# Order of the first loads, clears and copies in a chunked attention and top-1 MoE kernel

## The chip, the cores and the metric

One core of a Trainium2 chip runs the whole program. The metric is the device time of one execution in microseconds (us), smaller is better; the number quoted for the kernel before is the median of three runs. The engines of the core are TensorE (PE in the profile, with PEld for its weight loads), VectorE (DVE), ScalarE (ACT), GpSimd (POOL) and SyncE (SP, which here only issues DMAs).

## What is computed

Attention in chunks of 32 queries, each over 8 memory keys and a window of the sequence, and then a mixture of experts in which each token goes to one of eight:

```python
for c in range(S // 32):                      # B 4, H 8, S 768, D 64
    l, r = max(0, 32*c - 16), min(S, 32*c + 32 + 8)
    k_full = concat(mem_k, k[:, :, l:r]); v_full = concat(mem_v, v[:, :, l:r])
    a = softmax(q[:, :, 32*c:32*c+32] @ k_full.T / sqrt(D))
    out[:, :, 32*c:32*c+32] = a @ v_full
x = out.transpose(0, 2, 1, 3).reshape(3072, 512)
e = argmax(x @ w_gate + modality_bias[modality_id])   # softmax gives the gate
y = gate * (relu(x @ w1[e]) @ w2[e])
```

## The kernel before

**Tiling.** The 32 pairs of batch and head are taken two at a time: 16 units of two heads, here called pairs 0 to 15 (`u` in the code). Each pair is done in two halves of twelve chunks (`hf`). For each pair there are a key tile `kbd` (two of them in turn: `kbds`), in which both heads' transposed keys stand as blocks with zeros beside them, and a value tile `vw` (three in turn: `vws`), 128 partitions with rows 0 to 63 for head 0 and rows 64 to 127 for head 1. In `vw` 56 rows of a head hold the window of a chunk and 8 rows the memory values; the blocks in which the one head's rows meet the other head's columns stay zero. They are cleared once for each of the three tiles, `vws[0]` and `vws[1]` half by VectorE (L136) and half by GpSimd (L154, L845), `vws[2]` wholly by GpSimd (L866). `edge_v` (L274) writes the column of ones that gives the softmax's sum, with the first and the last chunk apart.

**Loads.** `load_qk(u)` (L97) issues the keys' and the queries' load of a pair, 384 KB each. `load_v(u)` (L283) issues four loads for each head: the main one (L290, 184 KB, elements of 256 bytes), two small ones for the ends (L291, L292) and the memory values (L294 or L297). For pair 0 the memory values come from DRAM, spread over the chunks by the load itself; from pair 1 on they come from `spread_v`, two tiles in SBUF that VectorE fills with `spread_mem` (L193): `spread_mem(0)` in the prologue at L197, `spread_mem(1)` within `more_constants`. `mkp`, `mvr` and other small inputs go through ScalarE's queue.

**A pair's steps.** `trans_k` and `store_k` transpose the keys into `kbd` (PE, then two copies of 64 partitions for each head on ScalarE and VectorE); `mem_keys` (L327) puts the memory keys in, two copies on GpSimd, from `memT`, which VectorE copies from a transpose of `mk` at L851. `regroup_q`, `trans_q` and `store_q` do the same for queries. `scores`, `less_max` (maximum and subtraction on VectorE), `exps_t` (transposes, then the exponential on ScalarE) and `attend` follow for each half, then `normalize` on VectorE and `trans_x`. Before `attend`, `share_v` (L299) copies 24 rows of each window to the next chunk's place: eight copies of six chunks on GpSimd, head 0's four first, then head 1's four. The first half of a pair attends over chunks 0 to 11.

**Order.** On PE, SP and GpSimd instructions run in the order in which the program writes them; during the attention stage so do those of ScalarE and VectorE. The prologue stands at L843 to L868, the loop over the 32 halves at L872 to L956. In the loop the half `i` computes its scores while the half `i - 1` attends; `load_qk(u + 3)` and `load_v(u + 2)` stand at the end of a pair's first half. `pump` puts single steps of routing and of the constants between VectorE's other instructions. After the attention comes the mixture of experts, matmul after matmul on PE to the end.

Of the kernel before, what the change touches and what calls it, by code (L numbers as in the profile page):

```python
# [9 lines left out]
F32 = mybir.dt.float32  # L10
# [10 lines left out]
P = 128  # L21
B, H, S, D = 4, 8, 768, 64
NMEM = 8
NCH = S // 32
# [28 lines left out]
def tile_chunk_attention_top1_moe(  # L53
# [14 lines left out]
    nc = tc.nc  # L68
# [14 lines left out]
    ld = c_ld.enter_context(tc.tile_pool(name="ld", bufs=3))  # L83
# [3 lines left out]
    qf = q.rearrange("b h s d -> (b h s) d")  # L87
    kf = k.rearrange("b h s d -> (b h s) d")
# [3 lines left out]
    def bank():  # L92
        return ps.tile([P, 512], F32, name="tr", tag="tr", bufs=4)

    q2s, k2s = {}, {}

    def load_qk(u):  # L97
        r0 = u * 2 * S
        q2s[u] = ld.tile([P, 2, 6 * D], F32, name="q2")
        k2s[u] = ld.tile([P, 2, 6 * D], F32, name="k2")  # L100
        for t, f in ((k2s[u], kf), (q2s[u], qf)):
            nc.sync.dma_start(t, f[r0:r0 + 2 * S].rearrange("(h p j) d -> p h (j d)", p=P, j=6))

    man = ExitStack()
    man.enter_context(tc.manual_schedule(engines={mybir.EngineType.Activation, mybir.EngineType.DVE}))
# [20 lines left out]
    vws = [pers.tile([P, 2, NCH, D + 1], F32, name=f"vw{i}") for i in range(NVW)]  # L126
# [3 lines left out]
    zero = const.tile([P, 1], F32, name="zero")  # L130
# [62 lines left out]
    def spread_mem(i):  # L193
        nc.vector.memset(spread_v[i][:, :, D:D + 1], 1.0)
        nc.vector.tensor_copy(spread_v[i][:, :, 0:D], mvr[:, i:i + 1].to_broadcast([P, NCH, D]))

    spread_mem(0)  # L197

    def more_constants():
        nc.vector.tensor_copy(iota, iota_i)  # L200
# [73 lines left out]
    def edge_v(i):  # L274
        t = vws[i]
        for h in range(2):
            r = slice(64 * h, 64 * h + 64)
            nc.gpsimd.memset(t[r, h, 1:NCH - 1, D:D + 1], 1.0)
            nc.gpsimd.tensor_copy(t[r, h, 0:NCH:NCH - 1], vedge[r])
# [3 lines left out]
    def load_v(u):  # L283
        vw = vws[u % NVW]
        for h in range(2):
            hh = 2 * u + h
            r0 = 64 * h

            src = bass.AP(tensor=vf.tensor, offset=(hh * S + 8) * D, ap=[[D, 32], [32 * D, NCH - 1], [1, D]])
            nc.sync.dma_start(vw[r0 + 24:r0 + 56, h, 0:NCH - 1, 0:D], src)  # L290
            nc.sync.dma_start(vw[r0 + 24:r0 + 48, h, NCH - 1, 0:D], vf[hh * S + S - 24:hh * S + S])  # L291
            nc.sync.dma_start(vw[r0 + 16:r0 + 24, h, 0, 0:D], vf[hh * S:hh * S + 8])  # L292
            if u == 0:
                nc.sync.dma_start(vw[r0 + 56:r0 + 64, h, :, 0:D], mvf[hh].unsqueeze(1).to_broadcast([NMEM, NCH, D]))  # L294
            else:
                m0 = NMEM * (hh % 16)
                nc.sync.dma_start(vw[r0 + 56:r0 + 64, h], spread_v[hh // 16][m0:m0 + NMEM])  # L297

    def share_v(u):  # L299

        vw = vws[u % NVW]
        for h in range(2):
            r0 = 64 * h
            for c in range(0, NCH - 1, 6):
                w = min(6, NCH - 1 - c)
                nc.gpsimd.tensor_copy(vw[r0:r0 + 24, h, c + 1:c + 1 + w, 0:D], vw[r0 + 32:r0 + 56, h, c:c + w, 0:D])  # L306

    def regroup_q(u):
# [13 lines left out]
    def store_q(u, j):  # L322
        if j == 0:
            qTs[u] = wk.tile([P, S], F32, name="qT")
        nc.scalar.copy(qTs[u].rearrange("p (s j) -> p s j", j=2)[:, :, j], qts.pop((u, j))[:, 0:384])

    def mem_keys(u, eng):  # L327
        for h in range(2):
            r = slice(64 * h, 64 * h + 64)
            eng.tensor_copy(kbds[u % 2][r, :, h, 56:64], memT[r, u:u + 1, :].to_broadcast([64, NCH, NMEM]))  # L330
# [13 lines left out]
    def store_k(u, h, j, copy):  # L344
        tt = kts[u, h][64 * j:64 * j + 64]
        win = bass.AP(tensor=tt.tensor, offset=tt.offset, ap=[list(tt.ap[0]), [16, NCH], [1, 28]])
        dst = kbds[u % 2][64 * h:64 * h + 64, :, h, 0:56]
        copy(dst.rearrange("p c (i j) -> p c i j", j=2)[:, :, :, j], win)  # L348
# [69 lines left out]
    def pump(k, pe=False):  # L418
        k *= KB if routing and routing[0][2] == B - 2 else 1
        while k > 0 and routing:  # L420
            g, wait, b, since = routing[0]
            if wait:
                if not pe or now[0] < since + (wait == "late" or b < B - 2) + (wait == "late" and b < B - 2):
                    return
                pe = False
            r = next(g, None)
            if r is None:
                routing.pop(0)
                return
            routing[0] = (g, r if r != "v" else "", b, now[0])  # L430
            k -= r == "v"
# [409 lines left out]


    edge_v(0)  # L843
    load_v(0)
    nc.gpsimd.memset(vws[1][64:P, 0], 0.0)  # L845
    edge_v(1)
    trans_k(0)
    t = bank()
    nc.tensor.transpose(t[:, 0:P], mk, ident)
    regroup_q(0)  # L850
    nc.vector.tensor_copy(memT.rearrange("p u m -> p (u m)"), t[:, 0:P])  # L851
    mem_keys(0, nc.gpsimd)
    for h in (1, 0):
        for j in range(2):
            store_k(0, h, j, nc.vector.tensor_copy if j else nc.scalar.copy)
    trans_q(0)
    for j in range(2):
        store_q(0, j)
    nc.vector.memset(kbds[1][0:64, :, 1], 0.0)
    load_qk(2)  # L860
    load_v(1)
    mem_keys(1, nc.gpsimd)
    share_v(0)
    nc.gpsimd.iota(iota_i, [[1, 192]], base=0, channel_multiplier=0)
    for h in range(2):
        nc.gpsimd.memset(vws[2][64 * h:64 * h + 64, 1 - h], 0.0)  # L866
    edge_v(2)
    load_v(2)  # L868

    units = [(u, hf) for u in range(NU) for hf in range(2)]  # L870
    n = len(units)
    for i in range(n + 2):  # L872
        live = i < n
        u, hf = units[i] if live else (NU, i % 2)
        now[0] = i
        if i == MAN:
            man.close()
        if live and i < n - 1:
            scores(u, hf)
        if 1 <= i <= n:  # L880
            exps_t(*units[i - 1])
        if live:
            less_max(u, hf)
            pump(1)
        if u + 1 < NU and hf == 0:
            trans_k(u + 1)
            regroup_q(u + 1)
            pump(3)
            store_k(u + 1, 1, 0, nc.scalar.copy)
            store_k(u + 1, 0, 0, nc.scalar.copy)  # L890
            store_k(u + 1, 0, 1, nc.scalar.copy)
            store_k(u + 1, 1, 1, nc.vector.tensor_copy)
            pump(3)
        elif u + 1 < NU:
            share_v(u + 1)
            if u + 2 < NU:
                mem_keys(u + 2, nc.gpsimd)
            trans_q(u + 1)
            store_q(u + 1, 0)
            store_q(u + 1, 1)  # L900
            pump(5)
        elif live:
            pump(5)
        first = i in (n - 3, n - 2)
        if first:
            trans_x(*units[i - 2])
        if i == n - 2:
            scores(*units[i + 1])
        if 1 <= i <= n:
            attend(*units[i - 1])  # L910
        if i == n:
            trans_x(*units[i - 2])
            trans(0)
            trans(1)
            conv(4)
            conv(5, nc.gpsimd)
            normalize(*units[i - 1])
            mm1(0)
        if i > n:
            mm1(1)  # L920
        if i >= 2 and not first and i != n:
            trans_x(*units[i - 2])
        if 1 <= i < n:
            normalize(*units[i - 1])
            pump(1)
        if i >= 2:
            u2, hf2 = units[i - 2]
            if hf2 == 1 and u2 % 4 == 3:
                routing.append((route(u2 // 4), True, u2 // 4, 0))
        if i == 1:  # L930
            routing.append((more_constants(), False, -1, 0))
        if i == 6:
            assert not routing
            bias_rows()
        if i < n:
            pump(1, True)
        if live and hf == 0:
            if u + 3 < NU:
                load_qk(u + 3)
            if u >= 1 and u - 1 + NVW < NU:  # L940
                load_v(u - 1 + NVW)
        if (u, hf) == (NU - 2, 1):
            while routing:
                pump(99, True)
            c_ld.close()
            xp = ctx.enter_context(tc.tile_pool(name="xp", bufs=1, side="right"))
            ix = xp.tile([P, 2], I32, name="ix")
            gx = xp.tile([P, 2], I32, name="gx")
            xg = [xp.tile([P, XW], F32, name=f"xg{t}") for t in range(2)]
            xth, xtl = [xp.tile([P, 4, 256 + NR], F32R, name=f"xt{i}") for i in range(2)]  # L950
            hh, hl = [xp.tile([P, 8, 256], F32R, name=f"h{i}") for i in range(2)]
            load_w(0, 0)
            gather(0)
        elif u == NU - 1:
            conv(2 * hf)
            conv(2 * hf + 1, nc.gpsimd)  # L956
# [165 lines left out]
```

## Time and profile before

| | us |
|---|---|
| median of three runs | 453.18 |
| lowest and highest run | 451.9, 453.71 |
| the profiled execution | 453.23 |
| its span, first to last instruction | 451.4 |
| PE busy | 422.2 |
| DVE busy | 312.6 |
| ACT busy | 260.4 |
| POOL busy | 199.3 |

The profile is one execution. Its span is 1.8 us shorter than that execution's time. "Busy" sums the time of an engine's instructions; an engine that is busy need not be the one that sets the end. In the time lines times are counted from the start of the span, and the bracket at a line's end is the idle time of that engine just before it and what ended it. The granted clock of TensorE is given as a share of its full 2.4 GHz; its lower level, 1.2 GHz, is 0.5.

### The profile page before, as it was taken

To read this page: it belongs to the slowest core of one execution; us is meant where nothing else is said; L and a number is where in the kernel's file an instruction comes from. 1 tells how busy PE (TensorE), PEld (TensorE's weight loads), DVE (VectorE), ACT (ScalarE), POOL (GpSimd) and SP (SyncE) were. 2 spreads that over 40 slices of the span, in tenths; PEclk is the share of its full clock that TensorE was granted. 3 is DMA by queue.
4 is the path that set the end of the run, shared out by engine and by line. 5 is a ranking of instruction groups with operands and counts; after the bars stand their busy time and mean duration, and the time that the engine had idled before them with its cause. 6 is when DMAs were issued, how large, how long until landed. Compare 5 with 4: busy or idle time off the path is not lost. (4 is left out here: it accounts for less than half of the span.)

```text
span 451.4 us, 11915 instructions
## 1 busy us (share of the span) xinstructions
PE 422.2 (94%) x4109; PEld 362.7 (80%) x4109; DVE 312.6 (69%) x756; ACT 260.4 (58%) x522; POOL 199.3 (44%) x376
## 2 busy tenths in 40 slices
PE   5979998998977898999999999999999999999993
PEld 2858786786756687989798998989898989898982
DVE  8699799799897699848456455857566675848430
ACT  5566776775646663747366455656565655657521
POOL 8977779789777833214042231313040404040201
PEclk9799999999999999999999999999999999999998
DMA  7798999999877502277187834202662201120101
GB/s 198 142 231 201 227 235 210 225 229 197 188 196 187 183 2 81 61 219 235 36 242 228 237 95 166 70 1 95 187 212 69 91 5 58 40 73 23 48 0 47
DMA packets 69570, 61.74 MB, mean 137 GB/s; under 512 B 30603, under 2 KB 59491, under 8 KB 69492
## 3 DMA queue, kind: packets, MB, share of 16 engines
q1 hardware_dynamic: 62480, 41.52, 37.8%
q0 software_dynamic: 5888, 19.11, 13.9%
q8 instruction: 36, 0.59, 0.6%
q14 instruction: 42, 0.34, 0.2%
q10 hardware_dynamic: 1124, 0.18, 0.2%
HBM read 76.02 MB, written 12.76 MB: 197 GB/s over the span
## 5 line engine op out<-in xcount | busy, mean ns | idle before, releaser
L778 PEld LDWEIGHTS tr<-xt,w 128*128 128x128 f32 x1152 | 141.0, 188 | 4.9 <-issue 2.7
L778 PE MATMUL tr<-xt,w 128*128 128x256 f32 (+1 forms) x1152 | 143.0, 284 | 1.9 <-PEq L1083 0.8
L788 PE MATMUL av<-wh,h 128*128 128x512 f32 x384 | 127.8, 399 | 0.0
L813 POOL DMA_INDIRECT out_dram<-o,ix_now x24 | 24.2, 1008 | 163.9 <-ACT o L809 161.9
L782 DVE SCALAR_TENSOR_TENSOR h<-tr,h 128x256 fp32r<-128x256 f32 x96 | 40.6, 423 | 71.6 <-ACT h L779 52.7
L788 PEld LDWEIGHTS av<-wh,h 128*128 128x128 f32 x384 | 72.3, 188 | 15.5 <-issue 0.4
L788 PE MATMUL av<-wl,h 128*128 128x512 f32 x192 | 75.6, 394 | 0.0
L306 POOL COPY vw<-vw 24x384 f32<-24x384 f32 (+1 forms) x128 | 61.0, 514 | 18.1 <-DMA vw<-in_v_dram 16.7
L725 DVE TENSOR_TENSOR wl<-raw,wh 128x512 fp32r<-128x512 f32 x91 | 63.0, 692 | 8.2 <-ACT wh L723 0.9
L779 ACT ACTIVATE h<-tr 128x256 fp32r<-128x256 f32 x96 | 36.8, 384 | 51.7 <-PE tr L778 30.5
L725 DVE TENSOR_TENSOR w<-raw,w 128x512 fp32r<-128x512 f32 x93 | 60.4, 695 | 5.0 <-ACT w L723 2.5
L723 ACT CAST wh<-raw 128x512 fp32r<-128x512 f32 x96 | 58.9, 615 | 2.0 <-DMA raw<-in_moe_w_dram 2.0
L723 ACT CAST w<-raw 128x512 fp32r<-128x512 f32 x96 | 53.6, 622 | 0.0
L809 ACT ACTIVATE o<-av,gate_now 128x512 f32<-128x512 f32 x24 | 16.2, 689 | 46.6 <-PE av L788 37.2
L788 PEld LDWEIGHTS av<-wl,h 128*128 128x128 f32 x192 | 36.2, 189 | 6.5
L348 ACT COPY kbd<-tr 64x672 f32<-64x672 f32 x47 | 36.6, 779 | 6.8 <-PE tr L342 5.8
L356 PE MATMUL sc<-kbd,qT 128*32 128x128 f32 x768 | 29.5, 290 | 2.9 <-POOL kbd L330 2.9
L740 POOL DMA_INDIRECT xg<-xd,gx x24 | 26.8, 1116 | 10.6 <-POOL gx L738 6.9
L376 ACT ACTIVATE PT<-tr 128x384 f32<-128x384 f32 x32 | 15.7, 492 | 25.8 <-PE tr L374 25.3
L386 PE MATMUL av<-vw,PT 128*32 128x130 f32 x768 | 28.3, 279 | 1.9 <-ACT PT L376 1.9
L761 ACT CAST xt<-tr 128x512 fp32r<-128x512 f32 x24 | 13.9, 587 | 24.3 <-PE tr L759 13.9
L356 PEld LDWEIGHTS sc<-kbd,qT 128*32 128x32 f32 x768 | 20.5, 115 | 8.4 <-issue 4.1
(245 smaller groups left out, 531.1 us busy)
## 6 DMA issues: line engine op xcount, KB each, us to landing
raw<-in_moe_w_dram SPq DMA_DIRECT2D x192, 256.0 KB
k<-in_k_dram SPq DMA_DIRECT2D x16, 384.0 KB
q<-in_q_dram SPq DMA_DIRECT2D x16, 384.0 KB
xd<-xb POOLq DMA_DIRECT2D x16, 384.0 KB, 5.6
vw<-in_v_dram SPq DMA_DIRECT2D x32, 184.0 KB
vw<-spread_v SPq DMA_DIRECT2D x30, 48.8 KB
vw<-in_v_dram SPq DMA_DIRECT2D x32, 6.0 KB
vw<-in_v_dram SPq DMA_DIRECT2D x32, 2.0 KB
```

Of the source, the lines that this page charges most:

```text
L306: nc.gpsimd.tensor_copy(vw[r0:r0 + 24, h, c + 1:c + 1 + w, 0:D], vw[r0 + 32:r0 + 56, h, c:c + w, 0:D])
L348: copy(dst.rearrange("p c (i j) -> p c i j", j=2)[:, :, :, j], win)
L356: nc.tensor.matmul(sc[32 * j:32 * j + 32, t * P:(t + 1) * P], qT[:, 32 * c:32 * c + 32], kbd[:, c].rearrange("p h m -> p (h m)"), start=Tr ...
L386: nc.tensor.matmul(avb[32 * j:32 * j + 32, t * W:(t + 1) * W], PT[:, t * P + 32 * j:t * P + 32 * j + 32], vw[:, :, c], start=True, stop=True,)
L723: nc.scalar.copy(wh[i], raw[i])
L725: (eng or nc.vector).tensor_sub(wl[i][:, s], raw[i][:, s], wh[i][:, s].bitcast(F32))
L740: nc.gpsimd.indirect_dma_start(out=xg[t], out_offset=None, in_=xd[0:rows], in_offset=bass.IndirectOffsetOnAxis(ap=gx[:, t:t + 1], axis=0))
L778: nc.tensor.matmul(pw, wt[f][:, c * P:(c + 1) * P], x[:, c, 0:w], start=(n == 0), stop=(n == 11))
L779: nc.scalar.activation(hh[:, f], ph, AF.Relu)
L782: nc.vector.scalar_tensor_tensor(hl[:, f], ph, 0.0, hh[:, f].bitcast(F32), op0=ALU.max, op1=ALU.subtract)
L788: nc.tensor.matmul(pos[t], x, w[8 + f], start=(f == 0 and n == 0), stop=(f == 7 and n == 2))
L813: nc.gpsimd.indirect_dma_start(out=out, out_offset=bass.IndirectOffsetOnAxis(ap=ix_now[:, t:t + 1], axis=0), in_=outs[t], in_offset=None, ...
```

## The change

In the prologue the order of the instructions changes:

- The keys of pair 2 are loaded ahead of the values of pair 0, its queries right behind these (both came together after the query copies of pair 0).
- On GpSimd `mem_keys(0)` comes ahead of the clearing of `vws[1]` and of `edge_v(1)`; `load_v(1)` follows `edge_v(1)`.
- The clearing of `vws[2]` is split: ScalarE clears rows 0 to 63 of head 1's columns by copying zeros, GpSimd the other half.
- `spread_mem(0)` leaves the prologue; it runs on VectorE in the loop's first pass, behind the key copies of pair 1, and `load_v(2)` is issued right behind it. Pair 1's memory values are therefore loaded from DRAM as pair 0's are.
- `share_v` alternates between the heads for each six chunks, in all pairs.

```diff
-    def load_qk(u):
+    def load_qk(u, parts=(0, 1)):
         r0 = u * 2 * S
-        q2s[u] = ld.tile([P, 2, 6 * D], F32, name="q2")
-        k2s[u] = ld.tile([P, 2, 6 * D], F32, name="k2")
-        for t, f in ((k2s[u], kf), (q2s[u], qf)):
-            nc.sync.dma_start(t, f[r0:r0 + 2 * S].rearrange("(h p j) d -> p h (j d)", p=P, j=6))
+        for i in parts:
+            tiles, f, name = ((k2s, kf, "k2"), (q2s, qf, "q2"))[i]
+            tiles[u] = ld.tile([P, 2, 6 * D], F32, name=name)
+            nc.sync.dma_start(tiles[u], f[r0:r0 + 2 * S].rearrange("(h p j) d -> p h (j d)", p=P, j=6))
...
-    spread_mem(0)
-
...
-            if u == 0:
+            if u < 2:
                 nc.sync.dma_start(vw[r0 + 56:r0 + 64, h, :, 0:D], mvf[hh].unsqueeze(1).to_broadcast([NMEM, NCH, D]))
...
-        for h in range(2):
-            r0 = 64 * h
-            for c in range(0, NCH - 1, 6):
-                w = min(6, NCH - 1 - c)
+        for c in range(0, NCH - 1, 6):
+            w = min(6, NCH - 1 - c)
+            for h in range(2):
+                r0 = 64 * h
                 nc.gpsimd.tensor_copy(vw[r0:r0 + 24, h, c + 1:c + 1 + w, 0:D], vw[r0 + 32:r0 + 56, h, c:c + w, 0:D])
...
     edge_v(0)
+    load_qk(2, (0,))
     load_v(0)
-    nc.gpsimd.memset(vws[1][64:P, 0], 0.0)
-    edge_v(1)
+    load_qk(2, (1,))
     trans_k(0)
...
     mem_keys(0, nc.gpsimd)
+    nc.gpsimd.memset(vws[1][64:P, 0], 0.0)
+    edge_v(1)
+    load_v(1)
     for h in (1, 0):
...
         store_q(0, j)
+    nc.scalar.copy(vws[2][0:64, 1], zero[0:64].unsqueeze(2).to_broadcast([64, NCH, D + 1]))
     nc.vector.memset(kbds[1][0:64, :, 1], 0.0)
-    load_qk(2)
-    load_v(1)
     mem_keys(1, nc.gpsimd)
     share_v(0)
     nc.gpsimd.iota(iota_i, [[1, 192]], base=0, channel_multiplier=0)
-    for h in range(2):
-        nc.gpsimd.memset(vws[2][64 * h:64 * h + 64, 1 - h], 0.0)
+    nc.gpsimd.memset(vws[2][64:P, 0], 0.0)
     edge_v(2)
-    load_v(2)
...
             store_k(u + 1, 1, 1, nc.vector.tensor_copy)
+            if u == 0:
+                spread_mem(0)
+                load_v(2)
             pump(3)
```

## Rows read from the trace of the kernel before

**Rows 1.** The page: PE's busy time, and its granted clock in 40 slices.
```profile
PE 422.2 (94%) x4109; PEld 362.7 (80%) x4109; DVE 312.6 (69%) x756; ACT 260.4 (58%) x522; POOL 199.3 (44%) x376
...
PEclk9799999999999999999999999999999999999998
```
**Rows 2.** Windows: stretch, busy time of each engine, PE's granted clock, DMA share, GB/s.
```profile
10.00:11.00 1.00, 0.00 (x0) 0.00 (x0) 1.00 (x1) 0.00 (x0) 0.81 (x4) 0.96 0.87 159
...
17.00:18.00 1.00, 1.00 (x7) 0.94 (x5) 0.56 (x1) 0.64 (x2) 0.96 (x2) 0.62 1.02 94
...
20.00:30.00 10.00, 8.60 (x156) 6.91 (x158) 9.66 (x39) 6.52 (x12) 9.55 (x21) 1.00 0.73 206
...
26.00:28.00 2.00, 1.42 (x28) 1.06 (x29) 1.96 (x9) 0.48 (x1) 1.88 (x6) 1.00 1.04 358
...
40.00:50.00 10.00, 10.00 (x176) 7.66 (x176) 8.46 (x23) 7.22 (x14) 5.86 (x12) 1.00 0.91 207
```
**Rows 3.** Time line of PE: start, duration, instruction, times; idle before it.
```profile
7.63 0.85 PE L320 MATMUL tr<-ident,qr 128*128 128x128 f32 x6 [1.01 <-DVE qr L311]
11.36 1.51 PE L356 MATMUL sc<-kbd,qT 128*32 128x128 f32 x24 [2.88 <-POOL kbd L330]
...
18.10 0.87 PE L386 MATMUL av<-vw,PT 128*32 128x130 f32 x24
...
24.33 0.87 PE L386 MATMUL av<-vw,PT 128*32 128x130 f32 x24
26.58 0.55 PE L408 MATMUL tr<-ident,xb 128*128 128x128 f32 x3 [1.38 <-DVE xb L401]
...
72.85 0.52 PE L408 MATMUL tr<-ident,xb 128*128 128x128 f32 x3 [1.64 <-DVE xb L401]
```
**Rows 4.** Time line of POOL, from the first edges to the second `share_v`.
```profile
7.87 0.29 POOL L279 COPY vw<-vedge 64x130 f32<-64x130 f32 x1
8.10 1.40 POOL L845 MEMSET vw<- 64x1560 f32 x1
...
10.57 1.54 POOL L330 COPY kbd<-memT 64x192 f32<-64x192 f32 x4
12.17 4.06 POOL L306 COPY vw<-vw 24x384 f32<-24x384 f32 x8
...
16.54 2.82 POOL L866 MEMSET vw<- 64x1560 f32 x2
...
20.45 4.83 POOL L306 COPY vw<-vw 24x384 f32<-24x384 f32 x8
```
**Rows 5.** Time line of DVE, the prologue, the third maximum and pair 5's queries.
```profile
6.03 0.92 DVE L195 COPY spread_v<-mvr 128x1536 f32<-128x1536 f32 x1
...
6.87 0.61 DVE L311 COPY qr<-q 128x768 f32<-128x768 f32 x1
...
7.71 1.75 DVE L348 COPY kbd<-tr 64x672 f32<-64x672 f32 x2
...
20.33 0.54 DVE L364 TENSOR_REDUCE mx<-sc 128x6 f32<-128x384 f32 x1
...
44.44 0.55 DVE L311 COPY qr<-q 128x768 f32<-128x768 f32 x1
```
**Rows 6.** Time line of ACT: the clearing of both key tiles, the first query copies.
```profile
2.54 2.84 ACT L134 COPY kbd<-zero 64x1536 f32<-64x1536 f32 x2
...
8.18 0.89 ACT L325 COPY qT<-tr 128x384 f32<-128x384 f32 x2 [0.59 <-PE tr L320]
```
**Rows 7.** Time line of SP, three of its DMA issues.
```profile
7.66 0.34 SPq L290 DMA_DIRECT2D vw<-in_v_dram  x1
...
13.36 0.28 SPq L292 DMA_DIRECT2D vw<-in_v_dram  x1
...
41.64 0.64 SPq L297 DMA_DIRECT2D vw<-spread_v  x1
```
**Rows 8.** Waits of SP from 4 to 27 us: in total, times, longest.
```profile
SPq L292 <- DMA vw<-in_v_dram: 0.5, 1, 0.5
```

## Prediction

> **What bounds the kernel now.** I read the page first: TensorE (PE) is busy 94% of the span and its clock falls below full only in the second of 40 slices, in the twelfth and in the last [rows 1]. The change touches only the first two of the sixteen head pairs, so the question is what sets the pace there, and whether time won there reaches the end. The view by windows answers the first half of it: the granted clock leaves 2.4 GHz within the 11th us (mean 0.96, so after about 0.92 of it) and comes back within the 18th (mean 0.62, so after 0.76 of it): some 6.8 us at 1.2 GHz, from 10.9 to 17.8 [rows 2]. VectorE (DVE) is busy 9.66 of the 10 us from 20 to 30; from 40 to 50 PE is busy all the time [rows 2].
>
> The time line of each engine then gives the chain. PE ends the first query transposes at 8.5, stands for 2.88 us until GpSimd (Pool) has put the memory keys into the first key tile, starts the first scores at 11.36, and gets to the first attend at 18.10 [rows 3]. Pool is late because `mem_keys(0)`, the first half of the four copies that start at 10.57, stands behind the clearing of `vws[1]` (1.40) and its edges, though what it needs, `memT`, is there by 7.71, where DVE's next instruction begins [rows 4, 5]. From 20.33 on DVE has hardly a pause, and PE waits for it at 26.58 [rows 2, 3, 5]. So: Pool's order until 11.4, PE at half clock until 18, DVE until about 40, PE after that. Whatever reaches DVE's row at 20.33 early reaches the end, unless a load is late.
>
> **The change part by part.**
>
> *The spread copy leaves DVE's front.* 0.92 us at 6.03 go [rows 5]. The regrouping of queries (0.61), `memT` (0.27, between the two rows shown) and two key copies (1.75) follow one behind the other, so the last copy ends at 9.46 - 0.76 = 8.7. ScalarE's two query copies (0.89, at 8.18 after 0.59 of idle) can start when ScalarE comes free at 7.6 and end by 8.6 [rows 6].
>
> *Memory keys first on Pool.* `edge_v(0)` ends at 8.16; `mem_keys(0)` is half of 1.54, 0.77 [rows 4]. It ends at 8.9, and the first scores start at 8.95 instead of 11.36: 2.4 us earlier. PE's pause of 2.88 shrinks to about 1.3. A pause of 1.38 (26.58) and one of 1.64 (72.85) left the clock at full [rows 1, 3], so I take it that it stays up. If it falls all the same, PE needs the 6.74 us that it needed before (11.36 to 18.10), and attends at 15.7.
>
> *Values and their copies.* What is swapped on Pool is a swap, so `share_v(0)` still starts near 12.17 [rows 4]. Its order changes: the second copy is now head 1's. In SP's time line the third value load of pair 1 stands still 0.5 us until 13.36, and what ends that is a value load [rows 7, 8]; I read it as head 1's main load of pair 0, the eighth issue before it. So Pool waits after one copy until 13.4. The third keys' load goes ahead of it: 384 KB that the DMA engines take over in a gap, since the values' issue at 7.66 waits for Pool's edges in any case, just as now [rows 4, 7]. I take 0.1 us for it; the bounds are 0 and the 1.1 us that these 384 KB need at the 358 GB/s of 26 to 28 us [rows 2]. One copy is 4.06 / 8 = 0.51. The first attend takes chunks 0 to 11, which are whole after four copies in the new order (six in the old): 13.5 + 3 x 0.51 = 15.0, at worst 16.1, against 18.10 now. With the half-clock case this is a gain of 2.0 to 3.1.
>
> *The spread copy in its new place* (0.92, on DVE, behind the last key copy of pair 1, about 12.8 to 13.7). Behind it on DVE stand the second maximum and subtraction, which PE wants after the first attend, so the Pool wait until 15.0 hides it; without that cover it costs 0.92. What the row of `share_v(1)` shows: eight copies took 4.83 instead of 4.06 where the other spread copy ran on DVE [rows 4], 0.77 more. The Trainium skill (SBUF — State Buffer, "Who interferes with whom") says of this that a DVE copy which uses both ports locks GpSimd out for the whole instruction, and speaks against the new place, beside the copies on which the attend now waits; the trace agrees with its 0.77. By the row the attend comes at up to 15.8, with a free Pool at 15.0; the copy lies mostly in Pool's wait for the load, so I take 0 and keep 0.77 as the bound.
>
> *DVE's chain.* The maximum at 20.33 starts 2.23 us after the first attend [rows 3, 5], which would make it 17.2. But between them stands the copy of `iota`, whose Pool half comes behind `share_v(0)`: 13.5 + 7 x 0.51 = 17.1, plus 0.2 between the rows at 12.17 and 16.54 for that instruction itself. With 0.4 for DVE's copies the maximum starts at 17.7: 2.6 us earlier. With the clock down it is 15.7 + 2.23 = 17.9, 2.4.
>
> *Pool later.* Half of the 2.82 us of clearing at 16.54 goes to ScalarE [rows 4]. Its cost there is half of 2.84, 1.42, behind the query copies (8.6 to 10.0) [rows 6]; next on ScalarE is the first key copy of pair 1, behind the first scores and the transposes after them, 8.95 plus half of 1.51 (half, at the full clock) and about as much again, 10.5: hidden, 0; uncovered, up to 1.4. Pool starts `share_v(1)` at 17.3 + 1.41 + 1.1 (edges: 20.45 less 19.36) = 19.8 instead of 20.45; four of eight copies (2.4) give 22.2 for the attend now at 24.33, half a microsecond after 24.33 - 2.6. PE's pause of 1.38 behind that attend covers it [rows 3].
>
> *Loads.* The pair-1 mem rows come from DRAM instead of the spread tile, 48 KB twice: between 0 and 0.4 us of DMA time, hidden before 19.8. The third values need Pool's clearing, which ends at 18.7 instead of 19.36 [rows 4], and the spread tile, ready at 13.7; the key loads behind them in SP's order move with them. From there on the DMA engines are full (share 1.04 from 26 us) [rows 2], so the stream of loads moves up by 0.7 us only while the engines move up by 2.6. The tightest load that I find is the query tile of pair 5: SP's wait for a query load ends at 41.64, DVE regroups at 44.44 [rows 5, 7]; 2.8 us of room, of which 1.9 is used. So the stream doesn't bind, but a gain over 3.5 would be cut there.
>
> **Sum.** 2.6 us, kept to the end: 453.23 of the profiled execution (span 451.4) - 2.6 = 450.6. The median of the runs is 453.18, so nothing has to be added.
>
> **The rivals.**
>
> *1. The clock falls in the new pauses and PE becomes the bound; slower.* From 11.36 to 18.10 PE did 6.74 us at half clock, so 3.4 at full; between 8.95 and the attend at 15.0 there are 6.05, so 2.7 us of pauses, and 3.8 if the third keys take their whole 1.1 us out of the values' time (attend at 16.1). After a pause of 2.88 the clock fell, after one of 1.64 it didn't, so it decides between these two [rows 3]. Another 6.8 us at 1.2 GHz then do 3.4 us less of PE's work: with the attend at 16.1 that is 3.4 - 2.0 = 1.4 us slower, 454.6, if nothing covers it. Against it: DVE is the bound from 20 on [rows 2], and covers most of it. What the rows show of the clock is that it fell after a pause and rose after steady work; the Trainium skill (TensorE: Matmul & The Clock Gate, "What's actually happening") has the low clock as the default which activity releases, and by that scattered pauses would count like one; no row here tells, and no chance rests on it.
>
> *2. The gain is eaten in part, 451.2 to 452.7.* The clock falls as above and DVE's queue covers most of the 3.4 us, not all; or the stream of loads bounds: if the third values come no earlier than now (first copies late by 0.7), engines that are 2.6 us ahead meet pair 5's queries with 0.2 us to spare, and every further slip is lost: gain 0.5 to 2. For it: full DMA engines; against it: from 40 to 50 us PE has no pause, so no load is late now [rows 2].
>
> *3. More than forecast, near 449.9.* If head 1's values land by 12.7, each step from there comes 0.7 us sooner: the attend at 14.3, the maximum at 17.0, the gain 3.3.
>
> *4. It doesn't do what it says:* scores still start at about 11 because another input is late (the query copies). Then only the 1.4 us of Pool clearing are left, off the path: 453.2. Against it, every other input is there at 8.7.
>
> **How the numbers follow.** Forecast 0.59, rival 1 0.06, rival 2 0.23, rival 3 0.07, rival 4 0.05. The forecast's own range is 450.1 to 451.2 (gain 2.0 to 3.1). For 8 in 10 I go to 449.4, half a microsecond past rival 3's time for what a second run differs, and to 452.5, into rival 2. A measurement of this kernel can tell about 0.5%, 2.3 us, from no change: the bound lies at 450.9. Of the forecast's 0.59 about 0.45 lies under it, with rival 3 0.52; slower by as much needs rival 1 at more than its price, 0.04; the rest, 0.44, is within.
>
> **What would show each step.** First scores near 9.0 and PE's pause before them near 1.3; PE clock at 1.00 from 10 to 20; `share_v(0)` with a wait for a value load after its first copy; first attend near 15.0; the maximum of pair 1 near 17.7; no query or value wait on PE or DVE at 40 to 50; all later rows shifted by about 2.6. Wrong if the clock falls, if the attend comes after 16.1, or if the shift is there at 20 us and gone at 50.

## The result, and the profile after

The changed kernel takes 456.21 us (median of 17 runs, 453.01 to 459.56) where the kernel before, run beside it, takes 451.9 (17 runs): a ratio of 1.0101, 95% interval 1.0082 to 1.0121. It is slower by 1%; the forecast was 450.6 us, 2.6 faster than before. The profiled execution took 456.09 us, its span 454.3 against 451.4 us before.

The page after, busy times and PE's granted clock in 40 slices, answers to [rows 1].

```profile
PE 425.7 (94%) x4109; PEld 365.5 (80%) x4109; DVE 316.2 (70%) x756; ACT 261.1 (57%) x523; POOL 201.0 (44%) x375
...
PEclk9889999998988999999999999999999999999998
```

Before, two slices stood below 9; now there are six, among them the 10th, 12th and 13th (102 to 114 and 125 to 148 us), far from the front. The mean granted clock is 0.978 of 454.3 us, so 10.0 us short of full; before it was 0.985 of 451.4, 6.8 us short. The difference, 3.2, is about the 2.9 us by which the spans differ.

The windows after (stretch, busy time of PE, PEld, DVE, ACT, POOL, PE's granted clock, DMA share, GB/s), beside [rows 2].

```profile
11.00:14.00 3.00, 3.00 (x34) 2.52 (x34) 2.84 (x7) 2.29 (x3) 1.02 (x3) 0.50 0.73 155
14.00:15.00 1.00, 1.00 (x9) 0.94 (x7) 1.00 (x1) 0.44 (x2) 0.94 (x2) 0.84 1.19 315
...
28.00:32.00 4.00, 4.00 (x39) 3.70 (x40) 3.52 (x17) 2.56 (x4) 3.64 (x8) 0.58 0.95 288
...
105.00:110.00 5.00, 4.33 (x44) 3.77 (x48) 4.14 (x11) 1.72 (x3) 4.68 (x8) 0.66 1.05 238
```

The first stretch at 1.2 GHz is half as long as before: it ends in the 15th us, not in the 18th. New ones lie within 28 to 32 and within 105 to 110, where the clock was full before.

PE's time line shows that the front did what the change is for.

```profile
9.74 0.86 PE L354 MATMUL sc<-kbd,qT 128*32 128x128 f32 x24 [1.86 <-DVE kbd L346]
...
15.11 0.65 PE L384 MATMUL av<-vw,PT 128*32 128x130 f32 x14
15.97 0.52 PE L384 MATMUL av<-vw,PT 128*32 128x130 f32 x9 [0.22 <-POOL vw L304]
...
27.12 0.86 PE L354 MATMUL sc<-kbd,qT 128*32 128x128 f32 x24 [0.53 <-POOL kbd L328]
...
111.88 0.86 PE L354 MATMUL sc<-kbd,qT 128*32 128x128 f32 x24
```

The same scores before:

```profile
27.05 0.86 PE L356 MATMUL sc<-kbd,qT 128*32 128x128 f32 x24
...
108.91 0.86 PE L356 MATMUL sc<-kbd,qT 128*32 128x128 f32 x24
```

The first scores come 1.6 us earlier than in [rows 3] and the first attend starts 3.0 us earlier, at 15.11, though ten of its 24 products come only from 15.97 on, behind a wait for a value copy. Then the gain goes: by 27 us nothing of it is left, and by 112 us PE is 3.0 us behind. DVE's time line has the first place (the copy of `iota` ahead of the third maximum, which was at 20.33 in [rows 5]):

```profile
18.41 1.53 DVE L198 CAST iota<-iota_i 128x192 f32<-128x192 int32 x1 [0.79 <-POOL iota_i L864]
...
20.06 0.54 DVE L362 TENSOR_REDUCE mx<-sc 128x6 f32<-128x384 f32 x1
```

Pool's time line has the second; it answers to [rows 4]. L304 is `share_v`, L328 `mem_keys`.

```profile
7.33 0.73 POOL L328 COPY kbd<-memT 64x192 f32<-64x192 f32 x2 [1.28 <-DVE memT L849]
...
11.75 0.50 POOL L304 COPY vw<-vw 24x384 f32<-24x384 f32 x1 [0.52 <-DMA vw<-in_v_dram]
13.70 4.32 POOL L304 COPY vw<-vw 24x384 f32<-24x384 f32 x7 [1.46 <-DMA vw<-in_v_dram]
18.09 0.29 POOL L864 IOTA iota_i<- 128x192 int32 x1
18.44 1.39 POOL L865 MEMSET vw<- 64x1560 f32 x1
...
21.70 4.58 POOL L304 COPY vw<-vw 24x384 f32<-24x384 f32 x8
26.33 0.73 POOL L328 COPY kbd<-memT 64x192 f32<-64x192 f32 x2
...
65.52 0.50 POOL L304 COPY vw<-vw 24x384 f32<-24x384 f32 x1 [1.27 <-DMA vw<-in_v_dram]
67.94 3.77 POOL L304 COPY vw<-vw 24x384 f32<-24x384 f32 x7 [1.92 <-DMA vw<-in_v_dram]
71.78 0.73 POOL L328 COPY kbd<-memT 64x192 f32<-64x192 f32 x2
```

The same pair in Pool's time line before, where the eight copies run through:

```profile
64.16 3.67 POOL L306 COPY vw<-vw 24x384 f32<-24x384 f32 x8 [1.68 <-DMA vw<-in_v_dram]
67.88 0.96 POOL L330 COPY kbd<-memT 64x192 f32<-64x192 f32 x2
```

Two things changed there. With heads in turn, Pool works four copies on the first head while the second head's load, issued last, is still landing; alternating, it makes one copy and stands: 1.92 us here, 0.22 to 1.46 in six other pairs, not at all in nine. And eight alternating copies that wait for nothing take 4.23 to 4.64 us (4.58 at 21.70), where those in turn took 3.67 to 4.06 in fifteen of the sixteen pairs before. So the values and the memory keys behind them, for which the scores of the next pair but one wait, come later, here by 3.9 us (71.78 against 67.88). Most of this lateness doesn't reach PE as a wait in this execution: between 10 and 147 us its waits for Pool sum to 1.1 us (0.5 for memory keys, 0.4 for the routing, 0.2 for values). What the alternation costs is therefore not read from this profile; the experiments show it.

### The profile page after: what moved, and what is told of

The parts are those of the page before. It is cut to its first block, busy times and chain, and to the rows that moved or that the text cites. A ratio compares the mean times of both kernels' runs of the same rounds, so it can differ in the third digit from the quotient of the medians.

```text
span 454.3 us, 11913 instructions
## 1 busy us (share of the span) xinstructions
PE 425.7 (94%) x4109; PEld 365.5 (80%) x4109; DVE 316.2 (70%) x756; ACT 261.1 (57%) x523; POOL 201.0 (44%) x375
## 5 line engine op out<-in xcount | busy, mean ns | idle before, releaser
L304 POOL COPY vw<-vw 24x384 f32<-24x384 f32 (+1 forms) x128 | 65.6, 513 | 17.8 <-DMA vw<-in_v_dram 11.9
L723 DVE TENSOR_TENSOR wl<-raw,wh 128x512 fp32r<-128x512 f32 x91 | 64.0, 704 | 8.7 <-ACT wh L721 1.3
```

Source lines behind the costliest of these rows:

```text
L723: (eng or nc.vector).tensor_sub(wl[i][:, s], raw[i][:, s], wh[i][:, s].bitcast(F32))
```

## The experiments

All ratios are against the kernel before, run beside each. "Short" is the profiled span times one minus its mean granted clock.

| kernel | ratio [95%] | median us | span us | clock | short us |
|---|---|---|---|---|---|
| after | 1.0101 [1.0082, 1.0121] | 456.21 | 454.3 | 0.978 | 10.0 |
| e1 heads in turn | 0.9986 [0.9961, 1.0011] | 453.18 | 453.1 | 0.985 | 6.8 |
| e2 alternating alone | 1.0134 [1.0102, 1.0166] | 460.13 | 459.9 | 0.974 | 12.0 |
| e3 iota first | 1.0107 [1.0077, 1.0137] | 458.38 | 457.1 | 0.977 | 10.5 |
| e4 in turn, iota first | 0.9986 [0.9960, 1.0013] | 451.83 | 447.4 | 0.994 | 2.7 |
| e5 second head first | 1.0102 [1.0068, 1.0136] | 457.27 | 453.3 | 0.983 | 7.7 |
| e6 large loads first | 1.0062 [1.0036, 1.0087] | 455.69 | 455.5 | 0.972 | 12.8 |
| e7 first pair alternates | 1.0027 [0.9997, 1.0057] | 454.56 | 453.6 | 0.980 | 9.1 |
| e8 fourth queries early | 0.9957 [0.9936, 0.9977] | 451.14 | 449.5 | 0.991 | 4.0 |
| e9 before, queries early | 1.0001 [0.9977, 1.0024] | 453.2 | 450.8 | 0.986 | 6.3 |
| e10 longer copies | 1.0103 [1.0068, 1.0138] | 457.71 | 458.0 | 0.981 | 8.7 |
| e11 keys ahead of copies | 1.0062 [1.0037, 1.0087] | 455.11 | 452.8 | 0.984 | 7.2 |
| e12 e8, keys ahead | 0.9945 [0.9922, 0.9968] | 450.37 | 450.0 | 0.987 | 5.9 |
| e13 e8, alternating | 1.0095 [1.0058, 1.0132] | 457.37 | 451.9 | 0.989 | 5.0 |
| e14 e6 and e11 | 1.0033 [1.0011, 1.0055] | 454.63 | 453.3 | 0.983 | 7.7 |

Single executions of one kernel spread over 1.8 to 7.8 us, and a profile is one of them: the profiled executions of e4, e5 and e13 were the fastest of theirs. The verdicts rest on the ratios, the rows only say where to look.

**Which part costs?** Theory A: alternating the heads. Theory B: the front, through `iota`. Theory C: chance falls of the clock.

e1, after with heads in turn, and e2, before with the loops of after:

```
 # e1 (after); e2 is the reverse edit of before
-        for c in range(0, NCH - 1, 6):
-            w = min(6, NCH - 1 - c)
-            for h in range(2):
+        for h in range(2):
+            for c in range(0, NCH - 1, 6):
+                w = min(6, NCH - 1 - c)
```

> The changed kernel with one part undone: the value copies take head 0's four first again, then head 1's. Theory A (the alternation costs it): with heads in turn Pool no longer stands inside a pair's copies until head 1's load is there (1.92 us at 66 us in the changed kernel), the one-hot tensors of routing on Pool come in time, and the kernel is 3 to 5 us faster than the changed one, no slower than the kernel before (ratio to before 0.997 to 1.003). Theory B (the front is to blame: iota behind the first value copies takes back what the front wins, and the load stream starts later): ratio stays near 1.010. Theory C (the clock falls once more, wherever pauses lie, near 105 us): ratio anywhere from 1.003 to 1.010, with the clock's fall still there in the profile.

> The kernel before with nothing but the alternation of heads in the value copies. Theory A: slower than before by 3 to 5 us (ratio 1.007 to 1.011), with waits of Pool inside a pair's copies. Theory B: no difference (0.998 to 1.002), since the front is that of before. Theory C: slower only if the profile shows the clock falling at a place where it doesn't fall in the kernel before.

e3, after with `iota` ahead of the first copies; e4 is e1 with the same edit:

```
     mem_keys(1, nc.gpsimd)
+    nc.gpsimd.iota(iota_i, [[1, 192]], base=0, channel_multiplier=0)
     share_v(0)
-    nc.gpsimd.iota(iota_i, [[1, 192]], base=0, channel_multiplier=0)
```

> The changed kernel with GpSimd's iota ahead of the first value copies instead of behind them. Theory B: the copy of iota on VectorE (1.53 us at 18.41, after 0.79 of waiting, in the changed kernel) starts right behind the first normalization at 17.6 and takes 0.25, so the third maximum starts at 18.0 instead of 20.06 and the whole is about 2 us faster than the changed kernel (ratio to before about 1.005). Theory A: the front wins the same 2 us, but Pool's lateness inside the pairs stays and takes it back by 80 us: ratio near 1.010.

> Both: heads in turn, and iota ahead of the first value copies, everything else as in the changed kernel. If A and B are both right this is the sum: 2 to 3 us faster than the kernel before (ratio 0.993 to 0.996), with the third maximum near 18 and all later rows that much earlier. If only A is right, ratio near 1.000; if neither, near 1.010.

Without the alternation nothing is lost (0.9986 twice); alternating alone costs 1.3%, more than the 1.1% that theory A allowed; moving `iota` under alternating copies saves nothing (1.0107). Theory A holds, B falls as the cause of the loss, and C falls as chance, since the loss comes and goes with the edit. PE's time line of e2 has one place at which it enters: the scores of the third pair wait for memory keys that stand behind the late copies of the second.

```profile
27.02 1.51 PE L356 MATMUL sc<-kbd,qT 128*32 128x128 f32 x24 [1.67 <-POOL kbd L330]
```

These scores are no later than before's, which started at 27.05 behind a wait for DVE. But in e2 the clock falls here, and the next scores start at 34.51 us instead of 30.79. The windows of 30 to 40 us, of before and then of e2, have the clock at 1.00 and at 0.67:

```profile
30.00:40.00 10.00, 8.91 (x169) 6.53 (x157) 9.44 (x27) 6.95 (x12) 6.94 (x14) 1.00 1.09 215
30.00:40.00 10.00, 9.79 (x125) 7.74 (x126) 5.57 (x16) 4.55 (x8) 6.37 (x13) 0.67 1.10 246
```

**Is it the wait for the second load, or the length of the copies?** e5 is before with the heads still in turn, the second first; its copies never alternate, but start only when the later load is there. e6 is e2 with both large loads of a pair issued ahead of the small ones. e10 is before with the last copy of each head made twice.

```
 # e5, in share_v
-        for h in range(2):
+        for h in (1, 0):
 # e10, in share_v
+                for _ in range(2 if w < 6 else 1):
                     nc.gpsimd.tensor_copy(vw[r0:r0 + 24, h, c + 1:c + 1 + w, 0:D], vw[r0 + 32:r0 + 56, h, c:c + w, 0:D])
 # e6, in load_v, behind the large transfer (L290)
+        for h in range(2):
+            hh = 2 * u + h
+            r0 = 64 * h
```

> The kernel before with one edit: GpSimd's value copies go head by head, but the second head's eight half first, whose load is issued last. The copies never alternate, but they now start only when the later load has landed, as the alternating ones do from their second copy on. Theory A1 (alternating costs through the wait for the second head's load): the ratio is near the 1.0134 of alternating alone, 1.008 to 1.014, about 457 to 460 us, with mid-run waits of 1 to 2 us on the load ahead of the first copy of a pair. Theory A2 (alternating costs because a copy takes 0.55 us instead of 0.46 when the next one lies in the other half of the partitions): the ratio is 1.000 +- 0.003, about 453 us, and a pair's eight copies take 3.7 to 4.1 us.

> The kernel before with alternating copies, and in every pair's value load the large transfers of both heads are issued first and the small ones behind them, so the second head's large transfer is issued some 1.6 us sooner. Theory A1 (the wait for the second head's load costs): most of the loss of 1.3 per cent goes, ratio 1.000 to 1.006, 453 to 456 us. Theory A2 (the copies' pace costs): ratio stays 1.010 to 1.016, 458 to 460 us.

> The kernel before, heads in turn, with the last value copy of each head (five columns of chunks instead of six) made twice, in every pair: about 2 x 0.4 = 0.8 us more of GpSimd per pair, some more than the 0.6 us by which eight alternating copies are longer than eight in turn, and no wait moved. It tells what the slower pace costs by itself. Theory A1 (the wait for the second head's load costs): ratio 0.999 to 1.004. Theory A2 (the copies' pace costs, as much or more): ratio 1.006 to 1.014, 456 to 460 us.

I held the wait for the cause and the length for harmless. e5 (1.0102) shows that the wait alone, without any alternation, costs 1.0%. e10 (1.0103) refutes the second half: longer copies alone cost as much. Its dose came out larger than meant, 4.64 to 5.12 us for ten copies where eight took 3.67 to 4.83 before, so it doesn't say how much of the 1.3% is the pace; e6, where part of the wait is gone and the pace is not, keeps 0.6%, just above the range that was set down for the wait as the cause. Either kind of lateness on Pool is paid. Pool's time line of the fourth pair, before and then e5: a wait of 4.15 us ahead of all eight copies instead of 2.04.

```profile
33.71 3.67 POOL L306 COPY vw<-vw 24x384 f32<-24x384 f32 x8 [2.04 <-DMA vw<-in_v_dram]
37.18 4.01 POOL L306 COPY vw<-vw 24x384 f32<-24x384 f32 x8 [4.15 <-DMA vw<-in_v_dram]
```

Pool's time line of e10, with what PE waited for between 10 and 147 us (releaser, us in total, times, longest):

```profile
22.23 5.12 POOL L307 COPY vw<-vw 24x384 f32<-24x384 f32 x10
```

```profile
PE sc L357 <- POOL kbd L331: 4.6, 3, 2.7
...
PE tr L681 <- POOL a L673: 2.9, 3, 1.3
```

Of the 4.6 us for memory keys 2.7 lie in the front, where before has its 2.88 [rows 3]. The other 1.9, in two waits, and the 2.9 for `a` are new.

**By which path does it reach PE?** The waits of e10 name two: the memory keys, and the one-hots `a` that Pool makes for the routing. e11 is e2 with `mem_keys(u + 2)` ahead of `share_v(u + 1)`; e14 is e6 with the same edit.

```
+            if u + 2 < NU:
+                mem_keys(u + 2, nc.gpsimd)
             share_v(u + 1)
-            if u + 2 < NU:
-                mem_keys(u + 2, nc.gpsimd)
```

> The kernel before with alternating copies, and the memory keys of the next pair but one put ahead of the value copies on GpSimd instead of behind them. Theory: late copies reach TensorE through the memory keys that stand behind them, for which the scores of the second next pair wait; then most of the loss of 1.3 per cent is gone, ratio 0.999 to 1.006. Rival: they reach it through the values themselves (the attend) or through the routing's work on GpSimd, and the order makes no difference: 1.010 to 1.016.

> The kernel before with alternating copies, both heads' large loads issued first and the memory keys ahead of the copies. If the two cures act on separate paths, the ratio is 0.998 to 1.003, 453 to 454 us. If they act on the same part of the loss, it stays at 1.004 to 1.008, 455 to 457 us, and the rest is in waits of TensorE on the values and on the routing's one-hots from GpSimd.

Each cure takes away about half of the 1.3% (1.0062 both, each interval clear of e2's; for e11 just outside the range that was set down for "most"). So the memory keys are one path and the wait for the load one source. The two together leave 1.0033, which lies between the two ranges set down for e14, and its interval overlaps those of e6 and e11: that the cures act on different parts is likely, not shown. What PE waited for in e11 names two candidates for the rest: the routing (`a`, L672), for which PE waits on Pool in none of before, e1, e4, e8, e9 and e12, and the keys' load, for which it never waits before:

```profile
PE tr L680 <- POOL a L672: 2.2, 2, 1.3
PE tr L338 <- DMA k<-in_k_dram: 2.0, 2, 1.7
```

That the rest goes these ways is read from such rows; no run isolated either.

**Where does the front's gain go when the heads are in turn?** The front wins 2 us and more, yet e1 and e4 are at 0.9986, which can't be told from before. In e1 DVE's time line has it: the queries of the fourth pair, loaded behind the third pair's values.

```profile
30.96 0.56 DVE L309 COPY qr<-q 128x768 f32<-128x768 f32 x1 [1.70 <-DMA q<-in_q_dram]
```

The windows of e1 show what follows, PE at 2.41 of 5 us and a clock of 0.79:

```profile
30.00:35.00 5.00, 2.41 (x28) 1.66 (x30) 3.77 (x12) 1.55 (x4) 0.87 (x3) 0.79 0.81 158
```

The profiled e4 had no such wait and kept its lead: its scores at 39.95 stood at 42.44 before, 2.5 us later. That is the forecast's mechanism, in one execution; its span of 447.4 is 4.0 us short of before's, and the 1.5 beyond the 2.5 come from later stretches. e8 is e4 with these loads issued first, at 19 us instead of 23; e9 is the same edit in before, ahead of the `load_v(2)` that stands above the loop.

```
             if u == 0:
                 spread_mem(0)
+                load_qk(3)
                 load_v(2)
...
-            if u + 3 < NU:
+            if 0 < u and u + 3 < NU:
                 load_qk(u + 3)
```

> The changed kernel with heads in turn and iota first, and the fourth pair's keys and queries issued ahead of the third pair's values instead of behind them (about 18 us instead of 23). Theory: with alternating gone, the front's gain of 2 to 2.5 us is lost in most executions because DVE waits for these queries near 30 us and TensorE's clock falls in the pause; then the early load keeps the gain in nearly all of them: ratio 0.993 to 0.996, 450 to 451 us against 453, and the time line shows no wait of DVE on queries at 29 to 31 us. Rival: the executions differ by chance elsewhere in the span; then the ratio stays near 0.9986.

> The kernel before with one edit: the fourth pair's keys and queries are loaded ahead of the third pair's values. Theory (the front's 2 us are what the reordered head wins, the early queries only stop it from being given back): the ratio is 1.000 +- 0.003, 453 us, because before's front is as late as ever. Rival (the early queries are themselves the gain, the reordered front is worth nothing): the ratio is that of the version with both, 0.993 to 0.997, 450 to 452 us.

e8 is faster than before, 0.9957, and its twelve runs lie within 450.46 to 453.07 where e4's lay within 449.22 to 455.17. In before the same early queries bring nothing (1.0001). So the front's gain is real, and worth 0.4% in e8. That it needs the early load is read from e1's row and from the narrower spread; e8 against e4 doesn't settle it, because their intervals overlap. DVE's time line of e8 at that place, without a wait:

```profile
29.61 0.56 DVE L309 COPY qr<-q 128x768 f32<-128x768 f32 x1
```

e13 puts the alternation back into e8 (the diff of e1 reversed); e7 is e4 with the first pair alone alternating, as below; e12 is e8 with the edit of e11.

```
-        for h in range(2):
-            for c in range(0, NCH - 1, 6):
+        cs = range(0, NCH - 1, 6)
+        for h, c in [(h, c) for c in cs for h in range(2)] if u == 0 else [(h, c) for h in range(2) for c in cs]:
```

> The changed kernel, alternating, with its iota ahead of the first value copies and the fourth pair's queries loaded early: only the alternation differs from the version at 0.9957. Theory: alternating costs its 1.0 to 1.4 per cent here too, ratio 1.006 to 1.010, 456 to 458 us, so the early queries alone would not have saved the change. Rival: alternating hurts mostly because it makes these queries late, and with them early the ratio is below 1.002.

> The changed kernel with GpSimd's iota ahead of the first pair's value copies, and alternating in the first pair alone; the other fifteen pairs go head by head. Theory: the loss of alternating collects over the pairs behind the first, where a late second load delays the memory keys that stand behind the copies; then the ratio is that of heads in turn throughout (0.9986), 450 to 453 us. Rival: the loss comes from the first pair, whose copies then push everything on GpSimd; then the ratio is 1.004 to 1.011, 455 to 458 us.

> The version with heads in turn, iota first and the fourth queries early (0.9957 of before), with the memory keys also ahead of the value copies on GpSimd. If late copies reach TensorE through the memory keys with heads in turn too, the ratio falls to 0.990 to 0.994; if the memory keys have slack there, it stays at 0.996 +- 0.003; if the memory keys, now waiting for the scores that read their buffer, hold up the copies behind them, it rises to 0.998 or more.

e13 is at 1.0095: the alternation costs 1.4% of e8, and early queries would not have saved the change. e7 lies between its two expectations (1.0027, interval 0.9997 to 1.0057), so how much the first pair alone costs stays open. But e7 and e3 differ only in the alternation of the other fifteen pairs, 1.0027 against 1.0107, and their intervals don't meet: these fifteen cost 0.8%. e12 (0.9945) can't be told from e8: with heads in turn the order of the memory keys shows no gain. It is the fastest median of all, 450.37.

## Why the prediction was wrong

*Where it failed: the alternation was priced in the first pair only.* The working follows `share_v(0)` and `share_v(1)`; the diff's loop order holds for all sixteen pairs. For the other fourteen nothing was set down, neither the wait after the first copy nor what stands behind the copies on Pool. Both were there to be read: the first pair's wait is in the prediction itself (until 13.4; it was 13.70), and the same order of issues, the second head's loads last, holds in each `load_v`. That Pool has little room in places stood in [rows 2], busy 9.55 of 10 us from 20 to 30 (5.86 from 40 to 50). Where the prediction put nothing, the runs showed that alternating costs 1.3% by itself (e2), and that the fifteen pairs behind the first cost 0.8% (e3 against e7). None of the rivals was this; the slower one was a clock fall in the front. The shift that the prediction wanted at 50 us was gone by 27, which is one of its own signs of being wrong.

*The pace of a copy* was taken from copies in turn: 4.06 / 8 = 0.51. The seven behind 13.70 took 4.32, 0.62 each: one of them took 1.11 beside the spread copy on DVE, for which the prediction took nothing (its bound was 0.77), and the median of the eight was 0.50 with a gap behind each. `share_v(0)` ended at 18.0, not 17.1, and `share_v(1)` began at 21.70, not 19.8. The part on Pool's later work ended with the attend; the memory keys of the third pair stand behind it, and PE waited for them (27.12).

*`iota` priced at 0.4.* It cost 0.79 of waiting and 1.53 for a copy of 0.25, so the third maximum came at 20.06, not 17.7: 2.3 us of the 2.6 were gone in this execution. It is a mis-sized term, not the cause: e3 took it away and lost as much.

*The tightest load was named wrongly.* It is the fourth pair's queries at 30 us, not the sixth pair's at 44. The rule used, that PE has no pause from 40 to 50, looked past the queries that DVE regroups at 31. Rival 2, the gain eaten by the stream of loads, fits e1's row with another place. It isn't what happened in the changed kernel, whose lead was gone by 27 us and whose DVE waited 0.27 us for these queries.

*What was right, and what was luck.* Right: `mem_keys(0)` first (7.33), the wait for the second head's load after one copy (13.70 against 13.4), and that the spread copy is hidden on DVE. The first attend at 15.11 against 15.0 is luck in part. The forecast had it wait for four copies; PE came to it without a pause, behind 3.4 us at 1.2 GHz, took the chunks that were whole, and then waited for the fourth copy until 15.97. The first scores came 0.8 later than forecast: the first key copies run on ScalarE, which issues loads of its own ahead of them and came to them at 7.05 instead of 6.06.

ScalarE's time line after:

```profile
7.05 1.52 ACT L346 COPY kbd<-tr 64x672 f32<-64x672 f32 x2 [1.67 <-PE tr L847]
```

Why the last of its issues moved from 5.66 to 6.65 was not tried. It cost the attend little, because the second part of it waited for the copies in any case.

*The clock.* The prediction also names a twelfth slice below full; [rows 1] have only the second and the last. After, the clock fell at 11 although PE's pause had shrunk to 1.86, so the forecast that it stays up was wrong for this execution; it came back 3.4 us earlier than before. With the same front it stayed at 1.00 until 20 us in the profiles of e1, e3, e4, e7, e8, e12 and e13, in e13 behind a pause of 1.99. So the length of that one pause, by which rival 1 was weighed, did not decide it. The slower end's 2.9 us lie beside 3.2 more of missing clock (10.0 against 6.8 short): the waits in the rows above, of 0.5 to 1.9 us, are followed by stretches with PE at 1.2 GHz. That one brings the other is read from the records and not isolated by a run; e10, only 1.9 us shorter of clock but 6.6 us longer than before, shows that it isn't all.

## What to carry to other kernels

A loop that is turned round for the sake of its first pass must be priced in all of its passes: look at the order in which its inputs are issued, because taking work in the order of landing hides the last load, and taking it by turns waits for it. On an in-order queue the cost of lateness is what stands behind, here the memory keys and the routing. When a front is moved up, list the next loads in time order and move the first that would be late with it; here neither half brought a gain clear of noise by itself (e4, e9), both together brought 0.4% (e8).

## What the runs showed of the hardware

- Pool copies of 24 x 384 in the same half of the partitions follow each other every 0.46 us where nothing disturbs them (3.67 for eight), by turns in the two halves every 0.53 to 0.58 (4.27 in e2, 4.23 to 4.64 after), though one copy has the same median, 0.50 in both. So in turn they overlap in the records, and by turns they stand apart. The change had been expected to cost nothing here.
- A DVE instruction that met Pool's clearing of 64 x 1560 (1.39 us) took as long as it: 1.53 for the copy of `iota`, an integer to float conversion that took 0.25 before. The prediction had the same page of the Trainium skill (SBUF — State Buffer, "Who interferes with whom") for the other direction. It says that whoever comes first holds the shared ports and the other waits, and lists cast and copy among those that can. This trace agrees that one waits for the other, for the cast with its 1.53; that the first comer is served it doesn't show, since the cast's record starts 0.03 us ahead of the clearing's. In e3 a reduction took 1.43 beside the same clearing, against 0.54 elsewhere:

```profile
17.65 1.65 DVE L639 COPY base<-iota 64x8 f32<-64x8 f32 x1
17.87 1.43 DVE L362 TENSOR_REDUCE mx<-sc 128x6 f32<-128x384 f32 x1
```

The page has it that a reduction never contends on this chip, and this row doesn't speak against it: the copy ahead of it on DVE, 0.19 before, was itself held until 19.30, and the reduction ended at the same time. A long record can be that of a neighbour's wait.
